# Drain buffers of one bank, one-hots in groups of tiles, and the order of loads and stores in a chunked attention with a mixture of experts

## The chip, the cores and the metric

One NeuronCore of a Trainium2 chip runs the whole program. The metric is the device time of one launch in microseconds (us), the median of several runs. Engines are named TensorE (PE; its weight loads PEld), VectorE (DVE), ScalarE (ACT), GpSimd (POOL) and SyncE (SP, which issues most of the DMAs). [...]

## The reference

Attention within chunks of 64 positions, for 8 batches, 8 heads, 576 positions and 64 dimensions; then a mixture of 8 experts over the 4608 tokens of 512 columns, for those tokens whose skip score is positive. Each token goes to its best expert alone:

```python
scores = scale * np.matmul(q_c, k_c.transpose(0, 1, 2, 4, 3))
attn = softmax(scores); x = np.matmul(attn, v_c)      # to (4608, 512)
xc = x[x @ w_skip > 0]
e_idx = np.argmax(xc @ w_gate, axis=1); gate_w = softmax(xc @ w_gate)[e_idx]
for e in range(8):
    h = np.maximum(xc[e_idx == e] @ w1[e], 0.0)       # 512 -> 1024
    y[e_idx == e] = gate_w * (h @ w2[e])              # 1024 -> 512
out = x.copy(); out[skip > 0] = xc + y
```

## The kernel before, in words

[...]

**Attention.** A loop (line 611) runs over 36 tiles of 128 tokens as a pipeline: in step i the scores of tile i+1 are computed (`pe_scores`, line 203) and their maximum taken (`ve_max`, line 214), tile i gets its exponential, tile i-1 its transpose and its product with v, tile i-2 its normalisation into x (line 258), tile i-3 is transposed again, scaled by ScalarE (line 290) and split into two float16 halves by GpSimd (`xh`, lines 292 and 293), and tile i-4 gets its routing logits on TensorE (lines 306 and 307). x is stored to `out` by SP (line 264); the stores of tiles from 23 on are held back until steps 34 and 35 and the code after the loop.

**Routing.** The tiles form three groups of 14, 9 and 13. When a group's logits are complete, a generator (`route`, line 323) yields its steps: kind "d" are VectorE steps with a cost, of which the loop takes some each tile (900 or 1100 ns, line 633), kind "p" TensorE steps. Each tile's one-hot of slots `oh` (line 396, VectorE, 128 x 128) and its record values `rv` (line 395, GpSimd; 88 columns a tile) go into matmuls that add up each expert's row records (line 413); `ohb` (line 387) is the one-hot of blocks. After group 1 the first three row blocks of the first expert are final and are gathered early by GpSimd's indirect DMA (line 470); after group 2 the rest.

**Weights.** W1 and W2 of the first expert come in 16 halves of 128 x 512 float32 (`load_half`, line 452), issued by SP in the steps that `W_TILES` (line 49) names: the eight halves of W1 in steps 23 to 30, those of W2 from 32 on. They pass through eight staging buffers (`wst`). `conv_half` (line 459) makes two float16 parts: ScalarE the first (line 462), GpSimd the second (a scaling, line 466, and a subtraction, line 467). Line 641 converts a half one step or more after it came. The other experts' weights are fetched four chunks ahead by `feed_load` (line 584; the DMA stands in line 576) through the same staging buffers, and converted by ScalarE and VectorE (lines 735 and 736).

**The drain.** After the loop (lines 650 to 714) the last tiles' steps are interleaved with the first layer of the first expert's first three blocks: `piece` (line 597) issues twelve matmuls over 384 columns for one eighth of the hidden columns, `evac` (line 604) its evacuation by ScalarE (line 495) and VectorE (line 496). Their PSUM comes from `sp_bank` (line 562), which hands out the two halves of tiles `sp` of two banks; two such tiles exist, shared with the scores of the loop. `early_xt` (line 568) transposes a gathered block. Before that code, line 650 calls `feed_load` once, ahead of the last five stores of x (lines 662 to 672). Lines 696, 697 and 704 to 706 are the last group's routing.

**The experts.** Units of row blocks follow, one expert after the other: layer two of a unit (line 520), with the next unit's gathers, transposes (line 483) and weights between its steps, then layer one of the next (line 491). Results are scattered by GpSimd (line 470).

Of the kernel before, what the change touches and what calls it, by code (L numbers as in the profile page):

```python
# [9 lines left out]
F32 = mybir.dt.float32  # L10
# [4 lines left out]
ALU = mybir.AluOpType  # L15
AX = mybir.AxisListType
PSUM = bass.MemoryType.PSUM

P = 128
# [4 lines left out]
DM = H * D  # L24
# [14 lines left out]
NG = len(GS)  # L39
# [3 lines left out]
NB = len(FLAT)  # L43
# [2 lines left out]
EMPTY = 5120.0  # L46

LOOK = 4
W_TILES = (23, 24, 25, 26, 27, 28, 29, 30, 32, 33, 33, 34, 34, 34, 35, 35)
W_ORDER = tuple((fc, part) for part in range(2) for fc in range(FC))  # L50
WSETS = 3
STB = 8
# [45 lines left out]
def moe_attention_kernel(ctx: ExitStack, tc: tile.TileContext, q: bass.AP, k: bass.AP, v: bass.AP, cst: bass.AP, wall: bass.AP, out: bass.AP):  # L98
    nc = tc.nc
    halves = (slice(0, CH), slice(CH, P))  # L100

    cpool = ctx.enter_context(tc.tile_pool(name="cpool", bufs=1))
# [2 lines left out]
    spool = ctx.enter_context(tc.tile_pool(name="spool", bufs=3))  # L105
    apool = tc.tile_pool(name="apool", bufs=2)
    ap = apool.__enter__()
    spool_ = tc.tile_pool(name="ps_s", bufs=2, space=PSUM)
    ps_s = spool_.__enter__()
    ppool = tc.tile_pool(name="ps_p", bufs=1, space=PSUM)  # L110
    ps_p = ppool.__enter__()

    man = tc.manual_schedule()
    man.__enter__()
# [51 lines left out]
    def C(name):  # L166
        lo, hi = _C[name]
        return csb[:, lo:hi]

    upper = cpool.tile([P, P], F16, name="upper")  # L170
    iota = cpool.tile([P, P], F16, name="iota")
# [5 lines left out]
    wgs = cpool.tile([P, KC, 2, NX], F16, name="wgs")  # L177
    reci = cpool.tile([P, NB], I32, name="reci")
    recg = cpool.tile([P, NB], F32, name="recg")
    onesf = cpool.tile([P, P], F32, name="onesf")  # L180
    nc.gpsimd.memset(onesf, 1.0)
    fixed = cpool.tile([P, 2, max(GS)], F32, name="fixed")
    nc.gpsimd.memset(fixed[:, 0], 1.0 / SGATE)
    nc.gpsimd.memset(fixed[:, 1], -0.498)
# [1 line left out]
    def more_constants():  # L186
        nc.vector.tensor_copy(upper, C("upper"))
        nc.vector.tensor_copy(iota, C("iota"))
        nc.vector.tensor_scalar(wgs[:, :, 0], wg, SR, None, op0=ALU.mult)
        nc.vector.scalar_tensor_tensor(wgs[:, :, 1], wg, SR, wgs[:, :, 0], op0=ALU.mult, op1=ALU.subtract)  # L190
        nc.gpsimd.tensor_copy(vals[:, :, 0], C("tok"))
        nc.gpsimd.tensor_copy(vals[:, :, 2], C("part").to_broadcast([P, NT]))
        nc.gpsimd.memset(ecum[:, 0, :], 0.0)
        nc.gpsimd.memset(rec, 0.0)
# [117 lines left out]
    def ve_logits(t):  # L312
        g, i, n = GT[t]
        if i == 0:
            lgs[g] = spool.tile([P, n, NX], F32, name="lg", bufs=3)
        nc.vector.tensor_reduce(lgs[g][:, i, :], T[t].pop("lp").rearrange("p (z n) -> p n z", z=2), axis=AX.X, op=ALU.add)
        if i == n - 1:
            r = route(g)
            routes.append([next(r), r])
# [3 lines left out]
    def route(g):  # L323
        n, t0 = GS[g], sum(GS[:g])
# [24 lines left out]
        vt = vals[:, t0:t0 + n, :]  # L349
# [31 lines left out]
        sl = spool.tile([P, n], F32, name="sl", bufs=2)  # L381
# [4 lines left out]
        ohb = ap.tile([P, n, NB], F16, name="ohb", bufs=2)  # L386
        nc.vector.scalar_tensor_tensor(ohb, C("kblk").unsqueeze(1).to_broadcast([P, n, NB]), 0.0, key.unsqueeze(2).to_broadcast([P, n, NB]), op0=ALU.add, op1=ALU.is_equal)
        rv = ap.tile([P, n, 4, NB], F16, name="rv", bufs=2)
        oh = ap.tile([P, n, P], F16, name="oh", bufs=2)
        for i in range(n):  # L390
            yield "d", 200
            s = slice(i, i + 1) if g + 1 < NG else slice(i, min(i + 7, n))
            sv = [P, s.stop - i, 4, NB]
            if g + 1 < NG or i % 7 == 0:
                nc.gpsimd.tensor_tensor(rv[:, s], ohb[:, s].unsqueeze(2).to_broadcast(sv), vt[:, s, :].unsqueeze(3).to_broadcast(sv), op=ALU.mult)
            nc.vector.scalar_tensor_tensor(oh[:, i, :], C("iota"), sl[:, i:i + 1], onesf, op0=ALU.is_equal, op1=ALU.mult)  # L396

        def sums():
            yield "d", 190
# [52 lines left out]
    def load_half(m):  # L452
        fc, part = W_ORDER[m]
        r = slice(part * DM, (part + 1) * DM)
        st = stpool.tile([P, DM], F32, name="wst")
        nc.sync.dma_start(st, wall[ORDER[0], fc, :, r])
        w_pend.append((st, fc, r))

    def conv_half(eng=nc.gpsimd):
        st, fc, r = w_pend.pop(0)  # L460
        w = wsets[0]
        nc.scalar.activation(w[:, 0, fc, r], st, AF.Copy, scale=SW)
        if eng is nc.vector:
            eng.scalar_tensor_tensor(w[:, 1, fc, r], st, SW, w[:, 0, fc, r], op0=ALU.mult, op1=ALU.subtract)
        else:
            eng.tensor_scalar(st, st, SW, 1.0, op0=ALU.mult, op1=ALU.mult)
            eng.tensor_tensor(w[:, 1, fc, r], st, w[:, 0, fc, r], op=ALU.subtract)
# [66 lines left out]
    def on(f, t, *a):  # L534
        if 0 <= t < NT:
            f(t, *a)
# [20 lines left out]
        for m in range(min(EARLY_B, ready[-1])):  # L557
            fetch(m, P * sum(GS[:EARLY_G]))

    spare = []  # L560

    def sp_bank():
        if not spare:
            t = ps_s.tile([P, 2, DM], F32, name="sp")
            spare.extend((t[:, 0], t[:, 1]))
        return spare.pop(0)

    def early_xt(m, alloc):
        blk_xt(xt0[:, :, :, m * P:(m + 1) * P], xgs[m], P, alloc)
# [1 line left out]
    def load_chunk(e, fc):  # L571
        st = [stpool.tile([P, DM], F32, name="wst") for _ in range(2)]
        for part in range(2):
            r = slice(part * DM, (part + 1) * DM)
            src = wall[e, fc, :, r] if isinstance(e, int) else wall[bass.ds(e, 1), fc, :, r].rearrange("o p w -> (o p) w")
            nc.sync.dma_start(st[part], src)
        return st
# [6 lines left out]
    def feed_load():  # L584
        while queue and len(pend) < STB // 2:
            p, fc = queue[0]
            if p >= WSETS and last[p - WSETS] >= unit[0]:
                return
            queue.pop(0)
            pend.append((p, fc, load_chunk(ORDER[p], fc)))  # L590
# [6 lines left out]
    def piece():  # L597
        if todo:
            fc = todo.pop(0)
            hp = sp_bank()[:, :N0]  # L600
            l1_mm(xt0, wsets[0], N0, hp, fc)
            evs.append((hp, fc))
# [8 lines left out]
    for i in range(-1, NT):  # L611
        host.clear()
        if i >= 0:
            on(load_q, i + LOOK)
            on(load_k, i + LOOK)
        for m in [m for m, t in enumerate(W_TILES) if t == i]:
            load_half(m)
# [21 lines left out]
        if i == 1:  # L639
            more_constants()  # L640
        if w_pend and (i > W_TILES[FC] or i < W_TILES[FC] and (len(w_pend) > 1 or i > W_TILES[FC - 1])):
            conv_half()
# [4 lines left out]
            run_route("rd", 1 << 30)  # L647
        early_fetch()

    feed_load()  # L650


    def conv():
        if w_pend:
            conv_half()

    host.clear()
    pe_ptrans(NT - 1)
    pe_xtrans(NT - 3, sp_bank)
    ve_norm(NT - 2)  # L660
    ac_pt(NT - 1)
# [5 lines left out]
    pe_logits(NT - 4)  # L667
    ve_logits(NT - 4)
    early_xt(EARLY_B - 1, sp_bank)
    pe_pv(NT - 1)  # L670
    ve_norm(NT - 1)
# [40 lines left out]
        evac()  # L712
    while w_pend:
        conv()
    apool.__exit__(None, None, None)
    ppool.__exit__(None, None, None)
    spool_.__exit__(None, None, None)
    bpool = ctx.enter_context(tc.tile_pool(name="bpool", bufs=1))
    ps_h = ctx.enter_context(tc.tile_pool(name="ps_h", bufs=3, space=PSUM))
    ps_x = ctx.enter_context(tc.tile_pool(name="ps_x", bufs=2, space=PSUM))  # L720
    ps_y = ctx.enter_context(tc.tile_pool(name="ps_y", bufs=3, space=PSUM))

    def xq_bank():
        return ps_x.tile([P, DM], F32, name="xq")
# [93 lines left out]
    for u, (p, bs, offs, n) in enumerate(units):  # L818
# [7 lines left out]
        w, hc = wsets[p], ht  # L826
# [38 lines left out]
    with tc.For_i(0, lend, 1) as si:  # L865
# [8 lines left out]
        for t in range(NT):  # L874
            oh = spool.tile([P, P], F16, name="ohx", bufs=2)
# [48 lines left out]
```

## Time and profile before

| | |
|---|---|
| median of 3 runs | 381.53 us (380.94 to 382.79) |
| the profiled execution, its own time | 381.37 us |
| its span | 379.6 us |
| TensorE busy | 327.1 us (86%) |
| VectorE, ScalarE, GpSimd busy | 245.6, 165.3, 152.2 us |
| mean granted clock of TensorE | 0.958 |
| moved by DMA | 81.83 MB, 216 GB/s on the mean |

All the views are of one profiled execution. The span runs from the first to the last instruction; the time also holds what lies around it. Busy shares are means over stages with different limits: the loop over tiles ends near 145 us, the drain near 182 us, the experts fill the rest. In a row of the timeline "[1.84 <-X]" says that the engine had been idle for 1.84 us and that X released it; "issue" is idle time for which the profile shows no releaser. SPq is SP's queue.

### The profile page before, as it was taken

What the parts mean: (1) busy time and instruction counts of PE and PEld (TensorE: products, weight loads), DVE (VectorE), ACT (ScalarE), POOL (GpSimd) and SP (SyncE); (2) the same over time, 40 slices, a digit from 0 to 9 for tenths busy, and PEclk for the clock granted to TensorE, in tenths of its full rate; (3) what the DMA queues carried; (4) which work ended last, traced back from release to release, by engine and by line L of the source; (5) the groups of instructions that cost most, each with busy time, mean ns of one, the idle gap of its engine ahead of it and who ended that gap; (6) DMA issues with size and microseconds to landing.
All of it is one profiled execution on the core that took longest, in us unless ns stands there. A gap on an engine that the chain in (4) does not pass through costs nothing.

```text
span 379.6 us, 11266 instructions
## 1 busy us (share of the span) xinstructions
PE 327.1 (86%) x4543; PEld 230.5 (61%) x4543; DVE 245.6 (65%) x552; ACT 165.3 (44%) x335; POOL 152.2 (40%) x195
## 2 busy tenths in 40 slices
PE   7777777878886767687999999899999999999991
PEld 3667666767775655453455555485674766769570
DVE  1554445779669826457554799887697777966520
ACT  2443433544555435321433572366365454645320
POOL 5154453568889986441712012502423124011111
PEclk9998998999989889986999999999999999999997
DMA  7999898998987961114474258767657867575000
GB/s 276 392 374 322 238 271 292 273 298 281 385 294 226 328 232 59 55 56 167 159 235 154 72 205 272 254 222 229 230 172 233 262 212 239 190 216 168 29 26 26
DMA packets 42472, 81.83 MB, mean 216 GB/s; under 512 B 5150, under 2 KB 5150, under 8 KB 42416
## 3 DMA queue, kind: packets, MB, share of 16 engines
q1 hardware_dynamic: 39168, 71.47, 57.0%
q0 software_dynamic: 3104, 9.33, 7.5%
q8 instruction: 37, 0.61, 0.6%
q10 hardware_dynamic: 144, 0.26, 0.2%
q14 instruction: 19, 0.16, 0.1%
HBM read 67.01 MB, written 14.17 MB: 214 GB/s over the span
## 4 chain that ended last, share of the span: by engine, by line
PE 70%; DVE 15%; issue 6%; ACT 4%; POOL 1%; DMA 1%; POOLq 0%; ACTq 0%; DVEq 0%
PE y L520 25%; PE hp L491 19%; PE sp L211 5%; DVE oh L396 5%; PE sp L491 4%; PE xt L279 4%; PE pv L248 4%; ACT xs L290 3%; PE xq L483 2%; DVE mx L216 2%; PE pt L233 2%; PE xt L306 2%; PE xt L162 1%; PE sp L222 1%; DVE x L258 1%
## 5 line engine op out<-in xcount | busy, mean ns | idle before, releaser
L520 PE MATMUL y<-wset,ht 128*128 128x512 f16 (+7 forms) x552 | 101.9, 379 | 0.0
L491 PEld LDWEIGHTS <-wset 128*128 128x128 f16 x864 | 74.9, 99 | 32.2 <-issue 12.8
L491 PE MATMUL hp<-xt,wset 128*128 128x288 f16 (+6 forms) x768 | 81.1, 267 | 1.8 <-DVE ht L496 1.1
L470 POOL DMA_INDIRECT out<-yo,reci x22 | 24.5, 1112 | 142.7 <-DVE yo L530 122.7
L520 PEld LDWEIGHTS <-ht 128*128 128x128 f16 (+7 forms) x552 | 45.6, 101 | 46.5 <-issue 2.0
L736 DVE SCALAR_TENSOR_TENSOR wset<-wst,wset 128x512 f16<-128x512 f32 x112 | 71.5, 683 | 1.4 <-ACT wset L735 0.8
L735 ACT ACTIVATE wset<-wst 128x512 f16<-128x512 f32 x112 | 63.0, 621 | 2.0 <-DMA wst<-in_wall 2.0
L290 ACT ACTIVATE xs<-xt 128x512 f32<-128x512 f32 x33 | 19.7, 596 | 61.3 <-PE xt L279 58.8
L495 ACT ACTIVATE ht<-hp 128x288 f16<-128x288 f32 (+6 forms) x64 | 23.6, 370 | 49.7 <-PE hp L491 49.4
L216 DVE TENSOR_REDUCE mx<-sp 128x8 bf16<-128x512 f32 x36 | 24.7, 687 | 24.9 <-PE sp L211 24.9
L496 DVE SCALAR_TENSOR_TENSOR ht<-hp,ht 128x288 f16<-128x288 f32 (+6 forms) x64 | 25.2, 404 | 22.6 <-ACT ht L495 21.5
L293 POOL TENSOR_TENSOR xh<-xs,xh 128x512 f16<-128x512 f32 x33 | 38.2, 1157 | 2.7
L292 POOL CAST xh<-xs 128x512 f16<-128x512 f32 x33 | 20.4, 617 | 42.3 <-ACT xs L290 42.2
L248 PE MATMUL pv<-v,pts 64*64 64x65 f32 x1152 | 27.4, 228 | 8.5 <-issue 8.1
L211 PE MATMUL sp<-qk 64*64 64x64 f32 x1152 | 27.7, 234 | 5.2 <-issue 4.6
L470 POOL DMA_INDIRECT xg<-out,reci x22 | 24.7, 1123 | 14.4 <-DMA out<-x 8.1
L248 PEld LDWEIGHTS pv<-v,pts 64*64 64x64 f32 x1152 | 23.1, 141 | 9.8 <-issue 9.2
L211 PEld LDWEIGHTS sp<-qk 64*64 64x64 f32 x1152 | 22.2, 143 | 8.5 <-issue 6.4
L484 ACT ACTIVATE xt<-xq 128x512 f16<-128x512 f32 (+7 forms) x19 | 9.6, 508 | 40.9 <-PE xq L483 40.9
L226 ACT ACTIVATE px<-sp 128x512 f32<-128x512 f32 x36 | 21.6, 600 | 11.5 <-PE sp L222 11.5
L258 DVE TENSOR_TENSOR x<-pv,rr 128x512 f32<-128x512 f32 x36 | 24.9, 691 | 1.2
L233 PE MATMUL pt<-ident,px 128*128 128x128 f32 x144 | 23.7, 291 | 1.4 <-ACT xs L290 1.4
(123 smaller groups left out, 387.5 us busy)
## 6 DMA issues: line engine op xcount, KB each, us to landing
wst<-in_wall SPq DMA_DIRECT2D x128, 256.0 KB, 3.6
v<-in_v SPq DMA_DIRECT2D x36, 260.0 KB, 4.6
qk<-in_q SPq DMA_DIRECT2D x36, 256.0 KB, 4.8
out<-x SPq DMA_DIRECT2D x36, 256.0 KB, 5.1
qk<-in_k SPq DMA_DIRECT2D x35, 256.0 KB, 5.3
xg<-out,reci POOLq DMA_INDIRECT x22, 5.3
out<-yo,reci POOLq DMA_INDIRECT x22, 4.0
qk<-in_k ACTq DMA_DIRECT2D x1, 256.0 KB, 3.8
```

Source lines behind the costliest of these rows:

```text
L211: nc.tensor.matmul(sp[halves[a], c, j * CH:(j + 1) * CH], qk[halves[c], 0, w], qk[halves[c], 1, w], start=(j == 0), stop=False, skip_group ...
L216: nc.vector.tensor_reduce(mx, T[t]["sp"][:, :, :KC * CH].rearrange("p c (j s) -> p c j s", s=CH), axis=AX.X, op=ALU.max, negate=True)
L233: nc.tensor.transpose(pt[:, j, :], px[:, j * P:(j + 1) * P], ident)
L248: nc.tensor.matmul(pv[halves[c], jj, m * VW:(m + 1) * VW], pt[halves[jj], c * 2 + jp, halves[a]], vv[halves[jj], c * KC + m, :], start=(m ...
L258: nc.vector.tensor_tensor(x.rearrange("p (g m d) -> p g m d", g=2, m=KC), pv[:, :, :, :D], rr.unsqueeze(3).to_broadcast([P, 2, KC, D]), op ...
L290: nc.scalar.activation(xs, T[t].pop("xt"), AF.Copy, scale=SX)
L293: nc.gpsimd.tensor_tensor(xh[:, 1], xs, xh[:, 0], op=ALU.subtract)
L470: ins = nc.gpsimd.indirect_dma_start(**kw)
L491: nc.tensor.matmul(hp, w[:, a, fc, j * P:(j + 1) * P], xt[:, b, j, :n], start=(m == 0), stop=(m == 11))
L520: nc.tensor.matmul(y[c * P // cg:c * P // cg + n], ht[:, a, fc, o:o + n], w[:, b, fc, P * KC:], start=(f == 0 and m == 0), stop=(f == fw - ...
L735: nc.scalar.activation(w[:, 0, fc, r], st[part], AF.Copy, scale=SW)
L736: nc.vector.scalar_tensor_tensor(w[:, 1, fc, r], st[part], SW, w[:, 0, fc, r], op0=ALU.mult, op1=ALU.subtract)
```

## The change

`sp_bank` takes its PSUM from a new pool of four tiles of one bank, `pd`, opened after the loop in the place of the pool of `sp`; the pool of `xt`, `pt` and `pv` is opened first so that it can outlive it, and the experts' pools are opened in another order (so in other banks). One-hots and record values are made for three tiles by one operation each, for seven in the last group, with an iota spread over the tiles instead of a scalar operand and the tile of ones. The call of `feed_load` ahead of the last stores is gone; the next call stands behind the last store. The eight halves of W1 are loaded in steps 6, 9, ... 27; line 641 then converts one in steps 9, 12, ... 27 and the last in step 28.

```diff
-W_TILES = (23, 24, 25, 26, 27, 28, 29, 30, 32, 33, 33, 34, 34, 34, 35, 35)
+W_TILES = (6, 9, 12, 15, 18, 21, 24, 27, 32, 33, 33, 34, 34, 34, 35, 35)
...
+    ppool = tc.tile_pool(name="ps_p", bufs=1, space=PSUM)
+    ps_p = ppool.__enter__()
     spool_ = tc.tile_pool(name="ps_s", bufs=2, space=PSUM)
     ps_s = spool_.__enter__()
-    ppool = tc.tile_pool(name="ps_p", bufs=1, space=PSUM)
-    ps_p = ppool.__enter__()
...
-    onesf = cpool.tile([P, P], F32, name="onesf")
-    nc.gpsimd.memset(onesf, 1.0)
...
-        for i in range(n):
-            yield "d", 200
-            s = slice(i, i + 1) if g + 1 < NG else slice(i, min(i + 7, n))
-            sv = [P, s.stop - i, 4, NB]
-            if g + 1 < NG or i % 7 == 0:
-                nc.gpsimd.tensor_tensor(rv[:, s], ohb[:, s].unsqueeze(2).to_broadcast(sv), vt[:, s, :].unsqueeze(3).to_broadcast(sv), op=ALU.mult)
-            nc.vector.scalar_tensor_tensor(oh[:, i, :], C("iota"), sl[:, i:i + 1], onesf, op0=ALU.is_equal, op1=ALU.mult)
+        step = 3 if g + 1 < NG else 7
+        for i in range(0, n, step):
+            s = slice(i, min(i + step, n))
+            w = s.stop - i
+            yield "d", 60 + 133 * w
+            sv, so = [P, w, 4, NB], [P, w, P]
+            nc.gpsimd.tensor_tensor(rv[:, s], ohb[:, s].unsqueeze(2).to_broadcast(sv), vt[:, s, :].unsqueeze(3).to_broadcast(sv), op=ALU.mult)
+            nc.vector.scalar_tensor_tensor(oh[:, s, :], C("iota").unsqueeze(1).to_broadcast(so), 0.0, sl[:, s].unsqueeze(2).to_broadcast(so), op0=ALU.add, op1=ALU.is_equal)
...
-    spare = []
-
     def sp_bank():
-        if not spare:
-            t = ps_s.tile([P, 2, DM], F32, name="sp")
-            spare.extend((t[:, 0], t[:, 1]))
-        return spare.pop(0)
+        return dpool.tile([P, DM], F32, name="pd")
...
-    feed_load()
+    spool_.__exit__(None, None, None)
+    dpool_ = tc.tile_pool(name="ps_d", bufs=4, space=PSUM)
+    dpool = dpool_.__enter__()
...
+    dpool_.__exit__(None, None, None)
+    ppool.__exit__(None, None, None)
     apool.__exit__(None, None, None)
-    ppool.__exit__(None, None, None)
-    spool_.__exit__(None, None, None)
     bpool = ctx.enter_context(tc.tile_pool(name="bpool", bufs=1))
+    ps_y = ctx.enter_context(tc.tile_pool(name="ps_y", bufs=3, space=PSUM))
+    ps_x = ctx.enter_context(tc.tile_pool(name="ps_x", bufs=2, space=PSUM))
     ps_h = ctx.enter_context(tc.tile_pool(name="ps_h", bufs=3, space=PSUM))
-    ps_x = ctx.enter_context(tc.tile_pool(name="ps_x", bufs=2, space=PSUM))
-    ps_y = ctx.enter_context(tc.tile_pool(name="ps_y", bufs=3, space=PSUM))
```

## Rows read from the trace of the kernel before

**Rows 1.** Busy time of each engine by stage: the stretch, its length, busy microseconds of PE, PEld, DVE, ACT and POOL with their instructions, then granted clock, DMA share and GB/s.

```profile
64.00:92.00 28.00, 23.12 (x639) 20.60 (x639) 22.65 (x64) 12.65 (x24) 17.53 (x30) 0.94 0.89 273
...
100.00:127.00 27.00, 19.74 (x521) 17.55 (x520) 22.05 (x59) 13.42 (x26) 24.27 (x35) 0.92 0.85 280
...
160.00:182.00 22.00, 17.26 (x88) 9.20 (x88) 13.59 (x39) 3.17 (x7) 8.15 (x10) 0.77 0.28 96
182.00:379.00 197.00, 186.82 (x1398) 117.87 (x1395) 136.80 (x253) 91.86 (x197) 44.83 (x40) 0.99 0.57 183
```

**Rows 2.** The chain that ended last, in order of time (start, length, what): its pieces on the one-hots of line 396.

```profile
83.41 0.94 DVE oh L396 x3
...
86.07 1.78 DVE oh L396 x5
...
89.57 1.94 DVE oh L396 x5
...
116.09 2.87 DVE oh L396 x5
...
120.68 3.05 DVE oh L396 x4
...
168.39 6.62 DVE oh L396 x13
```

**Rows 3.** Timeline of VectorE around `ohb` (start, length, operation), and the groups of `rv` on GpSimd by shape (count, busy us, mean ns).

```profile
81.97 1.43 DVE L387 SCALAR_TENSOR_TENSOR ohb<-csb,key 128x308 f16<-128x308 f32 x1
...
167.43 0.17 DVE L379 SCALAR_TENSOR_TENSOR bi<-rank,fixed 128x13 int32<-128x13 f32 x1
...
167.93 0.46 DVE L387 SCALAR_TENSOR_TENSOR ohb<-csb,key 128x286 f16<-128x286 f32 x1
...
L395 POOL TENSOR_TENSOR rv<-ohb,vals 128x88 f16<-128x88 f16 x23 | 7.9, 371 | 0.4 <-DVE ohb L387 0.4
...
L395 POOL TENSOR_TENSOR rv<-ohb,vals 128x616 f16<-128x616 f16 x1 | 1.2, 1212 | 3.9 <-DVE ohb L387 3.9
```

**Rows 4.** Timeline of GpSimd at the early gathers, and of TensorE at the logits behind them.

```profile
128.34 0.62 POOL L466 TENSOR_SCALAR wst<-wst 128x512 f32<-128x512 f32 x1
129.04 1.16 POOL L467 TENSOR_TENSOR wset<-wst,wset 128x512 f16<-128x512 f32 x1
130.37 1.26 POOL L470 DMA_INDIRECT xg<-out,reci  x1 [0.18 <-DVE ecum L427]
...
134.27 0.63 POOL L292 CAST xh<-xs 128x512 f16<-128x512 f32 x1
...
134.95 0.18 PE L306 MATMUL xt<-wgs,xh 128*128 128x18 f16 x1 [2.74 <-POOL xh L292]
136.18 0.19 PE L307 MATMUL xt<-wgs,xh 128*128 128x9 f16 x1 [1.05 <-POOL xh L293]
```

**Rows 5.** Timeline of TensorE in the drain, and VectorE's row for the block indicator `eh` of the last group.

```profile
148.83 0.66 PE L483 MATMUL sp<-ident,xg 128*128 128x128 f32 x4 [1.34 <-DVE xh L287]
...
154.81 2.11 PE L491 MATMUL sp<-xt,wset 128*128 128x384 f16 x12 [1.84 <-DVE ht L496]
...
162.65 3.28 PE L491 MATMUL sp<-xt,wset 128*128 128x384 f16 x12 [2.96 <-DVE ht L496]
165.73 0.31 PE L363 MATMUL xt<-eh,upper 128*128 128x117 f16 x1
...
166.57 4.20 PE L491 MATMUL sp<-xt,wset 128*128 128x384 f16 x24
...
172.96 2.36 PE L413 MATMUL xt<-rv,oh 128*128 128x88 f16 x9 [1.03 <-DVE oh L396]
175.53 6.49 PE L491 MATMUL sp<-xt,wset 128*128 128x384 f16 x24 [0.21 <-DVE ht L496]
181.85 3.40 PE L520 MATMUL y<-wset,ht 128*128 128x512 f16 x15
...
161.85 0.28 DVE L346 SCALAR_TENSOR_TENSOR eh<-csb,val 128x117 f16<-128x117 f32 x1
```

**Rows 6.** TensorE's waits for "issue" from 20 to 130 us (who waited for what: us in total, times, longest us), and the timeline's row of one of them.

```profile
PE pv L248 <- issue: 8.1, 6, 2.0
PE sp L211 <- issue: 4.6, 4, 1.9
...
101.11 0.34 PE L248 MATMUL pv<-v,pts 64*64 64x65 f32 x7 [1.10 <-issue]
```

**Rows 7.** Busy time by stretch in the drain, columns as in rows 1.

```profile
170.00:174.00 4.00, 2.16 (x13) 1.03 (x11) 4.00 (x8) 0.49 (x1) 2.59 (x3) 0.96 0.04 3
174.00:180.00 6.00, 5.75 (x21) 2.61 (x21) 3.52 (x14) 0.49 (x1) 0.00 (x0) 0.50 0.73 263
```

**Rows 8.** Timeline of SP's queue, of GpSimd and of ScalarE around the last stores and the gathers of the remaining blocks.

```profile
139.88 33.23 SPq L576 DMA_DIRECT2D wst<-in_wall  x8
173.20 2.79 SPq L264 DMA_DIRECT2D out<-x  x5
...
180.89 1.06 POOL L470 DMA_INDIRECT xg<-out,reci  x1 [8.13 <-DMA out<-x]
...
193.99 0.44 ACT L484 ACTIVATE xt<-xq 128x320 f16<-128x320 f32 x1 [7.22 <-PE xq L483]
```

## The prediction

> **What bounds the kernel now.** I read the busy time by stage first, then the chain of waits, then the timeline of each engine where the chain leaves TensorE. From 182 us on TensorE is busy 187 of 197 us [rows 1]: that half is bound by its matmuls, and nothing in the change shortens them. Before 182 us it is not: 17.3 of 22 us are busy from 160 to 182, and part of that at the lower clock (granted 0.77 on the mean) [rows 1]. Time can be won only there. The chain says what stands in the way: the one-hots of line 396 on VectorE in three places [rows 2], GpSimd from 100 to 127 us (24.3 of 27 us busy [rows 1]), and in the drain TensorE's waits for VectorE's evacuations [rows 5]. By half a per cent (1.9 us) and less this kernel's runs cannot be told from no change.
>
> **The sum's base.** The profiled execution took 381.4 us (span 379.6, 1.8 outside); the median of the three runs is 381.5, so I subtract from 381.4 and compare with either.
>
> **(a) One-hots of group 0, attention stage.** Fourteen operations become five (3, 3, 3, 3, 2 tiles). On the chain thirteen of the old ones took 0.94 + 1.78 + 1.94 = 4.66 us [rows 2], so fourteen some 5.0. The new form is that of `ohb` (an iota spread over one axis, a value over the other): 286 columns took 0.46 us, a 13-column operation 0.17 [rows 3], hence 0.17 us plus 1.06 ns a column. Three tiles are 384 columns, 0.56 us; two are 0.43. Five operations: 2.7 us, a gain of 2.3 if none is stopped. But an operation of VectorE with two SBUF inputs can stand behind GpSimd: `ohb` with 308 columns took 1.43 us while a subtraction of `xh` ran beside it [rows 3], 0.9 more than its own 0.5. I take 1.5 saved (0 to 2.3), nearer the free end because fewer operations meet fewer of GpSimd's.
>
> **(b) One-hots of group 1.** Nine in 2.87 + 3.05 = 5.92 us [rows 2]; they stood behind the W1 conversions too. Three new ones are 1.7 us of their own; with two stops of 0.6 they are 2.9. Saved 3.0 (1.2, if all three are stopped for 1.0, to 4.2). `rv` in threes on GpSimd goes from nine times 0.37 to three times 0.65 (88 columns 0.37, 616 columns 1.21, so 1.6 ns a column [rows 3]), 1.4 us less on the engine that is full there.
>
> **(c) W1's conversions leave GpSimd's full stretch.** Eight times 0.62 + 1.16 = 14 us of GpSimd move from tiles 24 to 31 to tiles 9 to 28 (one half every third tile, behind its load), where GpSimd was busy 17.5 of 28 us [rows 1]. What ends: the last conversion of W1 (until 130.2) stands ahead of the early gathers, which occupy GpSimd until 134.3, so the cast for tile 29 starts at 134.27 and TensorE's logits wait 2.74 + 1.05 us [rows 4]. With the gathers some 2 us and more earlier against the tiles, about 1 us of that wait is left. Saved 2.8 (0 to 3.8). In the tiles that now get a conversion, the cast of the next tile may start up to a microsecond late; a tile's logits follow one tile later, which covers that. Without the cover it would cost a microsecond in each of eight tiles.
>
> **(d) W1's loads at tiles 6 to 27.** Eight loads of 256 KB, each with one more issue in SP's queue, ahead of a store and of a load of v that is asked for four tiles early: nothing. They add 2.1 MB over some 80 us, 26 GB/s on 273 [rows 1]. What could pay is TensorE's stalls on "issue" in the middle of a run of matmuls, 8.1 + 4.6 us in ten places from 20 to 130 us [rows 6]: if each load lengthens one by its own transfer (256 KB at 300 GB/s, 0.87 us), 7 us; if they hide as the eight at tiles 23 to 30 did, 0, and those go away. I take 1.0 lost (0 to 7): the stall at 101 us, among the loads of before, was 1.10 us, no longer than others [rows 6]. [...]
>
> **(e) Drain: waits that come from shared tiles.** `sp_bank` deals out two halves of a two-bank tile. Three times TensorE waited to write one half until VectorE had read the other: 1.34 us at 148.83 (`early_xt` after the evacuation of tile 33's transpose), 1.84 at 154.81 (piece 1 after the evacuation of piece 0), 2.96 at 162.65 (piece 3 after that of piece 2) [rows 5]. With four tiles of one bank, a write waits only for the reader four calls back, which is long past in every case (piece 4 reuses piece 0's). The first two delay everything behind them: saved 3.2. The third stands in front of the ranking matmuls: `eh` is ready at 162.13, they start at 165.73, after the wait and a piece at half clock (3.28 us, against 2.11 at 154.81) [rows 5]. Freed, piece 3 runs while VectorE routes and is over when `eh` is. Saved 3.6.
>
> **(f) One-hots of the last group.** From the first operation at 168.4 [rows 2] to the last record matmul at 175.3 [rows 5] it is 6.9 us, 6.6 of them thirteen operations. Two operations of 896 and 768 columns are 1.11 and 0.97 us, GpSimd's two `rv` 1.21 and (528 columns, by the slope) 1.07 [rows 3]. Fully beside each other they need 2.3 us, one after another 4.4; the `ohb` row says that they stop each other, so I take 4.2, and 0.6 for the last six matmuls: 4.8. Saved 2.1 (1.9 to 4.0). GpSimd's last W2 conversion then comes behind both `rv`; the matmuls of layer two need it some 8 us later.
>
> **(g) Clock.** After the empty stretches before 162.6 and between 170 and 174 (2.2 of 4 us busy) the granted clock was 0.50, and pieces 6 and 7 took 6.49 us instead of the 4.20 of pieces 4 and 5 [rows 5, 7]. With (e) and (f) one gap of about 1.5 us is left ahead of the record matmuls. I take 1.5 of the 2.3 us (0 to 2.3).
>
> **(h) Stores ahead of the next expert's loads.** Eight loads sat in SP's queue for 33 us, waiting for staging buffers, and five stores behind them went out only at 173.2; the gathers then waited 8.1 us for the stores [rows 8]. Now the stores go as soon as x is there, and the loads queue behind the last of them. Saved on the chain: nothing. ScalarE had waited 7.2 us for the transposes of those gathers when they came at 193.99 [rows 8], because TensorE had layer two to do. The loads' price: the first of them move back behind the last store, the last still waits for the last conversion of W2, so all are on their way before layer two begins, and ScalarE converts from there on. If that cover failed, the conversions would start late by one landing: the last store was out by 176.0 and held the gather until 180.9, so some 5 us.
>
> **(i) Banks, `onesf`.** The later pools get the same numbers of banks; 0 (1 either way).
>
> Sum: attention -1.5 - 3.0 - 2.8 + 1.0 = -6.3; drain -3.2 - 3.6 - 2.1 - 1.5 = -10.4; in all -16.7, so **364.7 us**, 4.4% faster. All the rest moves earlier as a block.
>
> **Rivals.** *Drain only:* the attention stage gives its gain back, because TensorE's own tile with a stall is as long as the tiles that (a) to (c) shorten, or because (d) costs its upper bound. For: GpSimd and VectorE can take turns stopping each other with long operations as with short ones. Against: the chain runs through line 396 there [rows 2]. 381.4 - 10.4 = 371.0. *The change doesn't do what it says in the drain:* the waits of (e) belong to the order of the evacuations, not to the sharing of a tile, and come back on the new buffers with the clock. Against: pieces 4 and 5, which have no evacuation between them in program order, ran on without a wait in one tile [rows 5]. 381.4 - 6.3 - 2.1 = 373.0. *Slower:* the loads of (d) meet nearly full transfer queues (0.89 busy [rows 1]) and every code stall grows. To undo 16.7 and lose 2 more, each of the ten must grow by 1.9 us, from 1.3 to 3.2, and the price then is 384. It decides only beyond twice the mean stall; the longest of before is 2.0 [rows 6], with loads or without.
>
> **Chances.** Forecast (357 to 370) 0.66; drain only 0.15; waits stay 0.09; slower 0.06; nothing measurable 0.04. The first three are faster: 0.90; same 0.04; slower 0.06. All the terms at their good ends would give 358, at their bad ends 378; 357 to 374 takes in the forecast and the first two rivals and leaves out about 0.15.
>
> **What would show it.** Right: the waits of TensorE for line 496 before pieces 1 and 3 gone; five, three and two one-hot operations of about 0.56 and 1.0 us plus their stops; the gathers by 122 and the logits behind them waiting about 1 us; the first layer-two matmul near 165 instead of 181.85, at full clock; no gather waiting for `out`. Wrong: tiles 6 to 27 longer by more than 2 us in sum, pieces still waiting, or layer two starting later than 172.

## The result, and the profile after

| | before | after |
|---|---|---|
| median, with the result | 381.24 us (378.55 to 382.79) | 368.01 us (367.01 to 369.15) |
| ratio, with the result | | 0.966 [0.960, 0.973] |
| ratio, in two later sets of runs | | 0.955 [0.948, 0.961] and 0.956 [0.949, 0.962] |
| median of all 16 runs of after | | 366.6 us (362.3 to 369.2) |
| the profiled execution, its time and span | 381.37, 379.6 us | 367.09, 365.3 us |
| exponential of tile 35 begins | 144.70 us | 140.22 us |
| first matmul of layer two | 181.85 us | 167.43 us |
| from there to the end | 197.75 us | 197.87 us |

The kernel became 3.4 to 4.5% faster; 364.7 us was predicted and 366.6 is the median. The medians are of all executions; the ratios leave out those more than 1.5% above the fastest of their kernel. The rows of after have other line numbers, most of them two less: 209 and 246 are scores and product with v, 290 and 291 the float16 halves, 394 and 395 record values and one-hots, 469 gathers, 490 layer one, 519 layer two.

All of the profiled gain, 14.3 us, lies ahead of layer two, as forecast: 4.5 us until tile 35's exponential and 9.9 us from there to the first matmul of layer two (37.15 us before, 27.21 after). After that nothing changed (+0.1). Two later profiles of the same kernel divide the gain otherwise: 3.1 and 2.6 us until tile 35's exponential, and 12.3 from there to layer two (24.85 us).

Busy time by stage of the kernel after, columns as in [rows 1]:

```profile
64.00:92.00 28.00, 23.07 (x639) 20.60 (x632) 22.85 (x59) 13.29 (x26) 20.45 (x25) 0.94 0.92 302
100.00:127.00 27.00, 22.34 (x617) 19.68 (x608) 21.05 (x63) 12.64 (x24) 21.30 (x26) 0.94 0.80 262
136.00:140.00 4.00, 2.97 (x27) 2.65 (x27) 1.06 (x3) 0.88 (x2) 1.60 (x2) 0.54 0.52 199
140.00:146.00 6.00, 5.73 (x77) 4.79 (x78) 2.49 (x7) 3.33 (x7) 3.09 (x4) 0.50 0.20 74
146.00:167.00 21.00, 18.84 (x185) 12.43 (x178) 15.99 (x42) 7.45 (x16) 14.29 (x16) 0.99 0.34 107
167.00:365.00 198.00, 187.24 (x1401) 118.13 (x1399) 136.26 (x252) 91.33 (x196) 44.63 (x40) 0.99 0.56 183
```

GpSimd has 3.0 us less to do from 100 to 127 and 2.9 more from 64 to 92, and TensorE is busy 22.3 of those 27 us, no longer 19.7. In this profile the drain from 146 on runs at a granted clock of 0.99, where [rows 7] had 0.50; the low stretch now lies ahead of it, from 136 to 146 (0.54 and 0.50). The granted clock is TensorE's, as the share of its full speed that the profile gives; in the traces of before and after it is 1.00 or 0.50 at every moment from 7 us on, and a figure between them is a mean.

The chain that ended last, its rows on record values and one-hots and at its end (start, length, what), against [rows 2]:

```profile
83.37 1.78 POOL rv L394 x2
...
86.94 1.80 POOL rv L394 x2
...
114.94 2.31 DVE oh L395 x2
...
159.43 2.89 DVE oh L395 x2
...
163.69 3.90 PE pd L490 x24
167.59 11.65 PE y L519 x54
```

The one-hots of group 0 are off the chain, and GpSimd's record values (`rv`) have their place. The last group's one-hots fell from 6.62 to 2.89 us.

Timeline of TensorE, against [rows 4, 5]; the fourth row is a product with v that waited for "issue":

```profile
128.51 0.18 PE L304 MATMUL xt<-wgs,xh 128*128 128x18 f16 x1 [0.31 <-POOL xh L290]
...
129.75 0.18 PE L305 MATMUL xt<-wgs,xh 128*128 128x9 f16 x1 [1.05 <-POOL xh L291]
...
137.03 0.70 PE L246 MATMUL pv<-v,pts 64*64 64x65 f32 x12 [2.27 <-issue]
...
149.30 2.11 PE L490 MATMUL pd<-xt,wset 128*128 128x384 f16 x12
...
154.04 2.11 PE L490 MATMUL pd<-xt,wset 128*128 128x384 f16 x12
156.64 0.21 PE L361 MATMUL xt<-eh,upper 128*128 128x117 f16 x1 [0.49 <-DVE eh L344]
...
163.53 4.07 PE L490 MATMUL pd<-xt,wset 128*128 128x384 f16 x24
```

Pieces 1 and 3 (149.30 and 154.04) start without a wait; the ranking starts 0.06 us after `eh` is ready, not 3.6; pieces 6 and 7 take 4.07 us, not 6.49. Of the logits' wait behind the early gathers, 2.74 + 1.05 us, 0.31 + 1.05 is left.

Timeline of GpSimd, of SP's queue and of ScalarE, against [rows 4, 8]:

```profile
123.93 1.26 POOL L469 DMA_INDIRECT xg<-out,reci  x1 [0.32 <-DVE recg L434]
...
165.37 1.06 POOL L469 DMA_INDIRECT xg<-out,reci  x1 [0.16 <-DVE recg L434]
...
128.84 19.66 SPq L262 DMA_DIRECT2D out<-x  x9
148.59 51.34 SPq L570 DMA_DIRECT2D wst<-in_wall  x21
...
179.56 0.44 ACT L483 ACTIVATE xt<-xq 128x320 f16<-128x320 f32 x1 [8.31 <-PE xq L482]
```

The first early gather went from 130.37 to 123.93 (127.36 and 127.65 in the two later profiles); here it waits for the routing, no longer behind W1. The stores leave ahead of the loads, and the gather of the remaining blocks waits 0.16 us, not 8.13. ScalarE then waits 8.31 us for TensorE, where it waited 7.22: the earlier gathers bring nothing, as the forecast had it.

### The profile page after: what moved, and what is told of

It reads as the page before. It is cut to its first block, busy times and chain, and to the rows that moved or that the text cites. A ratio compares the mean times of both kernels' runs of the same rounds, so it can differ in the third digit from the quotient of the medians.

```text
span 365.3 us, 11225 instructions
## 1 busy us (share of the span) xinstructions
PE 322.1 (88%) x4543; PEld 229.2 (63%) x4543; DVE 237.7 (65%) x526; ACT 165.0 (45%) x335; POOL 152.8 (42%) x179
## 4 chain that ended last, share of the span: by engine, by line
PE 74%; DVE 9%; issue 7%; ACT 4%; POOL 4%; DMA 1%; POOLq 0%; ACTq 0%; DVEq 0%
PE y L519 26%; PE hp L490 20%; PE sp L209 5%; PE pv L246 5%; PE xt L277 4%; ACT xs L288 3%; PE pd L490 3%; PE xq L482 2%; PE xt L304 2%; PE pt L231 2%; DVE oh L395 1%; PE xt L162 1%; PE sp L220 1%; DVE mx L214 1%; DMA xg<-out,reci 1%
## 5 line engine op out<-in xcount | busy, mean ns | idle before, releaser
L490 PEld LDWEIGHTS <-wset 128*128 128x128 f16 x864 | 73.5, 98 | 24.2 <-issue 3.8
L288 ACT ACTIVATE xs<-xt 128x512 f32<-128x512 f32 x33 | 19.7, 596 | 58.7 <-PE xt L277 56.6
L246 PE MATMUL pv<-v,pts 64*64 64x65 f32 x1152 | 28.2, 230 | 8.7 <-issue 8.1
L224 ACT ACTIVATE px<-sp 128x512 f32<-128x512 f32 x36 | 21.6, 599 | 10.3 <-PE sp L220 10.2
```

Source lines behind the costliest of these rows:

```text
L246: nc.tensor.matmul(pv[halves[c], jj, m * VW:(m + 1) * VW], pt[halves[jj], c * 2 + jp, halves[a]], vv[halves[jj], c * KC + m, :], start=(m ...
L288: nc.scalar.activation(xs, T[t].pop("xt"), AF.Copy, scale=SX)
L490: nc.tensor.matmul(hp, w[:, a, fc, j * P:(j + 1) * P], xt[:, b, j, :n], start=(m == 0), stop=(m == 11))
```

## The experiments

The runs came in three sets, one under each of the next three headings, and each ratio is against the kernel before in the same set. The kernel after itself was run in the second set (label after_again: 364.71 us, 0.955 [0.948, 0.961]) and in the third (after_third: 366.59 us, 0.956 [0.949, 0.962]), not in the first.

### One part undone at a time

**u_banks**: the new pool, but two tiles of two banks dealt out in halves.

```diff
     def sp_bank():
-        return dpool.tile([P, DM], F32, name="pd")
+        if not spare:
+            t = dpool.tile([P, 2, DM], F32, name="pd")
+            spare.extend((t[:, 0], t[:, 1]))
+        return spare.pop(0)
...
-    dpool_ = tc.tile_pool(name="ps_d", bufs=4, space=PSUM)
+    dpool_ = tc.tile_pool(name="ps_d", bufs=2, space=PSUM)
```

> The changed kernel, with the drain's buffers again two tiles of two banks, each dealt out in halves. Theory (sharing a tile makes TensorE wait for the other half's reader): the waits before early_xt, piece 1 and piece 3 are back (1.3, 1.8 and 3.0 us) and the lower clock with them, 6 to 8 us slower than the changed kernel, about 375 us. Rival (the waits belong to the order of the evacuations): the same 368 us.

Measured: 373.07 us, 0.975 [0.968, 0.981]. Timeline of TensorE at `early_xt`, at pieces 1 and 3 and at layer two:

```profile
148.03 0.66 PE L482 MATMUL pd<-ident,xg 128*128 128x128 f32 x4 [1.34 <-DVE xh L285]
...
154.01 3.79 PE L490 MATMUL pd<-xt,wset 128*128 128x384 f16 x12 [1.83 <-DVE ht L495]
...
163.54 3.18 PE L490 MATMUL pd<-xt,wset 128*128 128x384 f16 x12 [2.97 <-DVE ht L495]
...
177.16 11.82 PE L519 MATMUL y<-wset,ht 128*128 128x512 f16 x54
```

All three waits [rows 5] are back, to a hundredth, with all the rest of the change in place, and every execution is longer than the six of after_again on the same chip (370.86 us or more against 366.74 or less). The waits belong to the sharing of a tile, not to the order of the evacuations.

**u_onehot**: the old one-tile one-hots and the tile of ones (the part of the change's diff on them, with its signs turned).

> The changed kernel with one one-hot operation a tile again (and the tile of ones). Theory: the last group's one-hots cost 2.7 us more on the chain, those of group 1 about 2 us, those of group 0 nothing; 4 to 6 us slower, about 373 us. Rival (grouping pays only where nothing else of VectorE waits, in the last group): 2.7 us, 370.7 us.

Measured: 371.22 us, 0.972 [0.965, 0.979]. Timelines of VectorE and of TensorE in the drain:

```profile
158.45 6.70 DVE L396 SCALAR_TENSOR_TENSOR oh<-csb,sl,onesf 128x128 f16<-128x128 f32 x13
...
165.25 6.06 PE L491 MATMUL pd<-xt,wset 128*128 128x384 f16 x24
171.14 11.82 PE L520 MATMUL y<-wset,ht 128*128 128x512 f16 x54
```

From tile 35's exponential (141.67) to layer two it is 29.47 us, against 24.85 in after_again and after_third: 4.6. About 2.7 us of it are the one-hots, and 2.0 come in pieces 6 and 7, which take 6.06 us instead of 4.07; the kernel before had 6.49 for them, at a granted clock of 0.50 [rows 7]. Tile 35's exponential itself is no later than in the kernel after (140.22 to 142.08): in groups 0 and 1 the old operations cost nothing that shows.

**u_w1**: `W_TILES` as before.

> The changed kernel with W1 loaded in steps 23 to 30 again, so converted in steps 24 to 31. Theory (the eight conversions on GpSimd hold up tiles 27 to 34): 4 to 6 us slower at step 34, 1.5 us of it given back in tiles 6 to 23; about 371.5 us. Rival (the one-hots in groups alone shortened those tiles): the same 368 us or a microsecond less.

Measured: 368.30 us, 0.965 [0.958, 0.971]. Tiles 27 to 35 (from exponential to exponential) take 36.99 us, against 31.1 to 33.6 in the eight profiles that convert W1 early: the conversions cost there what the theory said. Tiles 5 to 27 took 78.14 us, the shortest of all thirteen profiles (less_dma, below, aside), which more than gives it back; but that execution (364.4 us) was also the fastest of its six, and by the ratio u_w1 is some 3 us behind the kernel after.

**u_order**: `feed_load()` ahead of the last stores again.

> The changed kernel with the next expert's first eight loads issued ahead of the last stores again. Theory (the stores' place saves nothing on the chain, and the stores now fill the transfer queues while TensorE's code is fetched: a stall of 2.3 us at 137 us and the lower clock until 147): 2 to 5 us faster, about 364.5 us, and the stall of 137 us gone. Rival (the late stores held the gathers, and these the experts): 4 us slower, 372 us.

Measured: 365.15 us, 0.956 [0.950, 0.962], and 24.85 us from tile 35 to layer two. The order of stores and loads makes no difference that these runs can tell. Theory and rival fell: the time is that of the kernel after, and a stall at tile 34 is still there, 0.80 us long.

### What W1's place is worth, and the stall at tile 34

**after_again** is the kernel after.

> The changed kernel unchanged, as the measure for the other runs here and to see whether its stalls come at the same places in a second profile. Theory: about 368 us, and TensorE stalls on issue for about 2 us in the product with v of tile 34 again. Rival (the stall at 137 us was chance): no stall there, and the time spreads over 364 to 371 us.

Measured: 364.71 us (362.33 to 366.74), and the stall at tile 34 is there again, 1.32 us long.

**stored29**: the stores held back from tile 29 on, not from 23.

```diff
-STORED = 23
+STORED = 29
```

> The changed kernel with only the stores of tiles from 29 on held back (before: from 23 on); six stores move into steps 26 to 31, ahead of the loads of W2. Theory (TensorE's code stands behind the backlog of stores in the transfer queues at 128 to 137 us): the queues are empty earlier, no stall in tile 34's product with v and no lower clock until 147; 4 us faster than the changed kernel, about 364 us. Rival (the place of the stall is not set by the stores): the same as the changed kernel, or slower by what the six stores cost in tiles 26 to 31.

Measured: 365.25 us, 0.951 [0.944, 0.958]. The timeline of TensorE:

```profile
139.81 0.45 PE L246 MATMUL pv<-v,pts 64*64 64x65 f32 x12 [1.49 <-issue]
```

The stall ahead of tile 34's product with v stayed (2.27 us in the first profile of after, 1.32 in after_again, 1.49 in after_third), though fewer stores are held back until then. Their place doesn't set it; that theory fell.

**order_w1**: the order of the loads and `W_TILES` both as before.

```diff
-W_TILES = (6, 9, 12, 15, 18, 21, 24, 27, 32, 33, 33, 34, 34, 34, 35, 35)
+W_TILES = (23, 24, 25, 26, 27, 28, 29, 30, 32, 33, 33, 34, 34, 34, 35, 35)
...
+    feed_load()
```

> The changed kernel with the next expert's loads ahead of the last stores again and W1 in steps 23 to 30 again, so with only the buffers and the one-hots changed. Theory (W1's place gives in tiles 27 to 34 what it takes in tiles 6 to 27): as fast as with the order alone undone, about 364.5 us. Rival (the two interact: W1's late loads make the backlog of the stores longer): 3 us slower than that.

Measured: 370.35 us (366.52 to 375.05), 0.966 [0.957, 0.974], some 4 us above u_order by the ratio. The theory that W1's place gives back what it takes fell; and since u_w1, with the new order, is at 0.965, the order adds nothing to it.

**loads_only**: W1 loaded in tiles 6 to 27, but converted in tiles 24 to 31.

```diff
-        if w_pend and (i > W_TILES[FC] or i < W_TILES[FC] and (len(w_pend) > 1 or i > W_TILES[FC - 1])):
+        if w_pend and (i > 32 or 24 <= i < 32):
```

> The changed kernel with W1 loaded in steps 6 to 27 but converted in steps 24 to 31, as before. Theory (tiles 6 to 27 pay for the loads, by TensorE's stalls on code, and tiles 27 to 34 for the conversions on GpSimd): it pays both, 3 to 5 us slower than the changed kernel, about 372 us. Rival (the early conversions are what tiles 6 to 27 pay for): as W1 late, about 368 us.

Measured: 370.64 us (369.22 to 373.51), 0.972 [0.966, 0.979]. Timelines of GpSimd and of TensorE, and last TensorE's wait of 129.06 as after_again has it:

```profile
129.08 1.16 POOL L466 TENSOR_TENSOR wset<-wst,wset 128x512 f16<-128x512 f32 x1
130.42 1.26 POOL L469 DMA_INDIRECT xg<-out,reci  x1 [0.18 <-DMA wst<-in_wall]
...
134.32 0.63 POOL L290 CAST xh<-xs 128x512 f16<-128x512 f32 x1
...
129.06 0.38 PE L220 MATMUL sp<-mx,identb 128*128 128x256 bf16 x2 [2.04 <-DVE mx L214]
...
135.00 0.18 PE L304 MATMUL xt<-wgs,xh 128*128 128x18 f16 x1 [2.92 <-POOL xh L290]
...
136.23 0.19 PE L305 MATMUL xt<-wgs,xh 128*128 128x9 f16 x1 [1.05 <-POOL xh L291]
...
128.47 0.38 PE L220 MATMUL sp<-mx,identb 128*128 128x256 bf16 x2 [0.46 <-DVE mx L214]
```

This separates loading from converting. All six runs are longer than all six of after_again on the same chip (362.33 to 366.74), and the medians are 5.9 us apart: converting early is what W1's place brings. The rows at the gathers are those of [rows 4] again, to 0.2 us. Loading early by itself brings nothing: order_w1, which loads late, is at 0.966, and the intervals overlap. In the profiles layer two starts at 170.42 and 170.94 us in these two, and at 166.50 in after_again.

### Single parts, and code against transfers

**after_third** is the kernel after.

> The changed kernel once more, as the measure for this set: between 364 and 368 us.

Measured: 366.59 us (362.87 to 368.26), as expected.

**last7**: groups 0 and 1 tile by tile, the last group in sevens.

```diff
-        step = 3 if g + 1 < NG else 7
+        step = 1 if g + 1 < NG else 7
```

> The changed kernel with groups 0 and 1 in operations of one tile (new form) and only the last group in sevens. Theory (the chain through the one-hots in tiles 28 to 32 was VectorE and GpSimd stopping each other once a pair): 3 to 4 us slower than the changed kernel, most of it in tiles 27 to 33. Rival (those tiles were held by the conversions of W1 alone, and the one-hots pay in the last group alone): the same time as the changed kernel.

Measured: 365.88 us, 0.955 [0.949, 0.961], the same as the kernel after. One-hots and record values of group 1 in its timeline, of VectorE and of GpSimd:

```profile
116.11 2.74 DVE L395 SCALAR_TENSOR_TENSOR oh<-csb,sl 128x128 f16<-128x128 f32 x5
120.49 1.75 DVE L395 SCALAR_TENSOR_TENSOR oh<-csb,sl 128x128 f16<-128x128 f32 x3
...
117.99 1.63 POOL L394 TENSOR_TENSOR rv<-ohb,vals 128x88 f16<-128x88 f16 x5
```

Eight one-hots take 4.49 us here. The same group's three operations took 2.31 us (the first two, on the chain above) and 0.55 in the kernel after:

```profile
118.89 0.55 DVE L395 SCALAR_TENSOR_TENSOR oh<-csb,sl 128x384 f16<-128x384 f32 x1
```

The grouping spares VectorE 1.6 us and the ninth operation, and the end does not move: in these tiles that work does not set the time.

**banks_only**: the kernel before with the one-bank buffers and the order of the pools, and nothing else.

> The kernel before with the one-bank buffers (and the order of the pools) alone. Theory (the waits on the other half are 6 to 8 us with their clock, whatever the rest): 6 to 8 us faster than before. Rival (without the shorter one-hots the last group's routing takes the gain back, since TensorE then waits there): 3 us or less.

Measured: 375.59 us, 0.979 [0.972, 0.985], 8 us by the ratio: the theory held. The timeline of TensorE, pieces 1, 3, 6 and 7:

```profile
151.54 2.11 PE L491 MATMUL pd<-xt,wset 128*128 128x384 f16 x12
...
156.28 2.11 PE L491 MATMUL pd<-xt,wset 128*128 128x384 f16 x12
...
168.38 6.71 PE L491 MATMUL pd<-xt,wset 128*128 128x384 f16 x24
174.93 11.82 PE L520 MATMUL y<-wset,ht 128*128 128x512 f16 x54
```

From tile 35's exponential (144.80) to layer two it is 30.13 us, 7.0 less than before. Pieces 6 and 7 are as slow as before (6.71 us, then 6.49), while u_banks, with the shorter one-hots but tiles shared in halves, has 4.07: these pieces are shortened by the one-hots, not by the buffers.

**less_dma**: odd tiles from 7 on take q, k and v of the tile before instead of loading their own; its time as a whole says nothing, since the routing becomes another.

```diff
-        if t < NT:
+        if t > 5 and t % 2 and t < NT:
+            T[t]["qk"] = T[t - 1]["qk"]
+        elif t < NT:
```

> The changed kernel with the loads of q, k and v left out in every odd tile from 7 on (the tile before it is used again, so its x and the routing differ and the time after the attention stage says nothing). Theory (TensorE's stalls on issue are its code standing behind data in the transfer queues): with three eighths of the traffic gone the stalls after tile 7 fall from some 12 us to under 4, and the exponential of tile 27 comes by 100 us instead of 107 to 110. Rival (a stall is a fixed cost of passing from one block of code to the next): the stalls stay at 1 to 2.5 us each, at the same matmuls.

Busy time from 30 to 100 us, of after_third and then of less_dma:

```profile
30.00:100.00 70.00, 56.22 (x1503) 49.79 (x1502) 41.98 (x114) 32.01 (x61) 45.11 (x54) 0.90 0.91 294
```

```profile
30.00:100.00 70.00, 60.31 (x1756) 52.92 (x1755) 50.71 (x137) 37.87 (x73) 52.87 (x63) 1.00 0.73 246
```

TensorE's waits in that stretch (who waited for what: us in total, times, longest), of after_third and then of less_dma:

```profile
PE sp L209 <- issue: 5.3, 3, 3.4
PE pv L246 <- issue: 3.0, 2, 2.2
PE xt L277 <- issue: 2.0, 1, 2.0
```

```profile
PE pv L250 <- issue: 2.3, 4, 1.1
PE sp L213 <- issue: 0.6, 1, 0.6
```

With the transfers' share down from 0.91 to 0.73, TensorE's stalls on "issue" fall from 10.3 to 2.9 us, the granted clock is 1.00 instead of 0.90, and tile 27's exponential begins at 97.9 us, where after_third has 110.6. In these two profiles the stalls are larger with more transfers beside them; the rival of a fixed cost for each fell, since no stall of this stretch is longer than 1.1 us in less_dma, against 3.4 in after_third.

The packets of an instruction queue come ahead of these stalls. This is the queue's row in the profile of the kernel after (packets, MB, share); the trace also has the times of each packet:

```profile
q8 instruction: 37, 0.61, 0.6%
```

From 20 to 145 us all the fourteen profiles together have 145 stalls of TensorE on "issue". Of these, 138 end 1.2 to 1.7 us after a packet of this queue has landed, all ten of the kernel before and all twelve of the first profile of after among them (1.26 to 1.58 us); with some 21 packets in that stretch of each profile, about one in ten would by chance (an estimate from these counts). By that the stalls are taken here for waits on TensorE's code. Eight to 13 stalls come to 20 to 23 packets (ten to 22 before, twelve to 21 after): about half of the packets have no stall behind them.

## Why the prediction held, step by step

The sum was -16.7, and the runs give -13 to -17 (0.966 to 0.955). That it came so near is in part luck. The attention part was forecast at -6.3 and came to -4.5, -3.1 and -2.6 us in the three profiles of the kernel after; the drain was forecast at -10.4 and came to -9.9, -12.3 and -12.3. One error made up for the other. The mechanisms held in the drain; the attention part gained by other terms than the forecast named. Layer two was forecast to begin near 165 us and began between 164.4 and 167.4 in the profiles of the changed kernel and of those as fast.

**(e) The shared tiles: right.** Predicted -6.8. The three waits are gone after, all three return in u_banks, and the buffers alone make the drain 7.0 us shorter (8 by the ratio of banks_only). The rival that the waits belong to the order of the evacuations fell.

**(f), (g) The last one-hots and the clock: right, a little small.** Predicted -2.1 and -1.5. From the end of `ohb` to the last record matmul it is 4.26 us (159.43 to 163.69), 6.93 before: -2.7. The two operations and GpSimd's `rv` hold each other up, as assumed from the `ohb` row [rows 3] (1.43 us there): they take 2.97 and 3.67 us. Timelines of VectorE and GpSimd of the kernel after:

```profile
156.30 0.28 DVE L344 SCALAR_TENSOR_TENSOR eh<-csb,val 128x117 f16<-128x117 f32 x1
...
158.97 0.46 DVE L385 SCALAR_TENSOR_TENSOR ohb<-csb,key 128x286 f16<-128x286 f32 x1
159.34 2.97 DVE L395 SCALAR_TENSOR_TENSOR oh<-csb,sl 128x896 f16<-128x896 f32 x2
...
159.57 3.67 POOL L394 TENSOR_TENSOR rv<-ohb,vals 128x616 f16<-128x616 f16 x2 [0.49 <-DVE ohb L385]
```

The first row is `eh`, from whose end the ranking's 0.06 us is counted. By the slopes of [rows 3], an estimate, the last two needed 2.1 and 2.3 us each for themselves, 4.4 one after another; together they end after 3.9. The clock's part is put at 2.0 to 2.4 us, by pieces 6 and 7: 6.49 us before, at a granted clock of 0.50 [rows 7], and 6.06 in u_onehot, against 4.07 after, where it is 0.99. In sum the drain is 12.3 us shorter in after_again and after_third (24.85 against 37.15), where 10.4 was predicted. In the first profile it is only 9.9: there the granted clock stood at 0.50 from 136 to 146, about the stall of 2.27 us that ended at 137.03, where after_third has 1.00.

**(a), (b) One-hots of groups 0 and 1: the step that failed.** Predicted -1.5 and -3.0. Group 1's operations did become 3.1 us shorter (5.92 to 2.86), just the size forecast, but last7, which has them tile by tile, is as fast as the kernel after, and u_onehot, with the old operations, reaches tile 35's exponential as early. The forecast took their place on the chain of waits [rows 2] for their worth. The chain says what was last at each step; what is next behind it the rows of that chain don't say. In group 0 it was GpSimd's `rv`, 1.78 and 1.80 us in the chain after; the forecast had named this itself as what speaks for the rival, and for these tiles that rival was true.

**(c) W1's conversions: right in kind, half the size.** Predicted -2.8, which came out of one wait, that for the gathers [rows 4]. Measured by loads_only against after_again: -5.9 in the times, -3.9 in the profiles (layer two at 170.42 and 166.50). Tiles 27 to 35 take 37.97 and 31.23 us, 6.7 less, and two tiles hold it. From tile 33's exponential to tile 34's it is 8.49 and 4.36 us: the gathers' wait is 2.92 us against 0.44, and behind it, at 136.51, the 32 matmuls of a tile's scores take 1.13 us in loads_only, where they took 0.69 at 129.64 (the granted clock is 0.87 in the mean from 120 to 141). From tile 31's to tile 32's it is 6.20 and 3.44: TensorE waits 2.04 us for `mx`, against 0.46. VectorE comes late to it: of its routing steps there, one of 128x3 (`reci`) took 0.74 us in the kernel before, beside a W1 subtraction of GpSimd, and 0.24 in the first profile of the kernel after. The forecast priced the conversions at the gathers alone and put the rest of these tiles' time down to (b). Tiles 5 to 27, where the conversions now lie, take 83.70 and 86.24 us, 2.5 more; yet that stretch spreads from 83.8 to 86.8 us among kernels that are alike up to there, and from 78.1 to 85.3 among those that convert late, so what the conversions cost there is not shown.

**(d) W1's loads: little, the size open.** Predicted +1.0 (0 to 7). loads_only loads early, order_w1 and u_w1 load late, and all three convert late: 0.972, 0.966 and 0.965, with overlapping intervals. That fits 0 to 3 us; 7 was not reached. (The 300 GB/s behind that 7 was the forecast's estimate; 273 GB/s at a DMA share of 0.89 [rows 1] come to 307.) TensorE's stalls on "issue" from 30 to 130 us come to 10.0 to 12.6 us in the four profiles that load late and 10.7 to 14.1 in the nine that load early: 1.1 more in the mean, within the spread. One of the forecast's own signs of being wrong did come: tiles 6 to 27, from exponential to exponential, took 79.40 us before and 80.96, 83.45 and 82.81 in the three profiles after. Four kernels that load and convert late spread from 75.35 to 82.50 over the same tiles, so the runs do not say whether the loads, the conversions or neither did that. About half of the code packets have a stall behind them, single stalls last up to 3.4 us (after_third), and in less_dma their sum from 30 to 100 us is 7.4 us smaller, at a DMA share of 0.73 instead of 0.91. So the rival that every stall grows with the traffic is borne out by less_dma, but eight loads of 256 KB did not move the stalls beyond their spread.

**(h), (i): right.** u_order shows no difference; the later pools' banks show none after 167 us (187.24 us busy in 198, before 186.82 in 197).

**What the forecast had not seen** is the stall at tile 34. It is in six of the eight profiles that convert W1 early (0.80 to 2.31 us), each time ahead of the last twelve matmuls of the product, and in none of the five that convert late. In four of the five the logits of the tile before wait long for the gathers (2.92 + 1.05 us in loads_only), and no stall follows at tile 34; the two early profiles without the stall, u_banks and u_onehot, have a wait of 2.87 us for ScalarE's `xs` in tile 32. That such waits cover it fits these six. But u_w1 has 1.07 + 0.43 us there, no more than after_again with 0.44 + 1.05, so what places the stall stays open. Nor is there a version clearly faster than the change: stored29, u_order and last7 lie within its interval.

## What to carry to other kernels

A row on the chain of waits is not yet the worth of shortening it: (b) was credited with 3.0 us by that chain, and undoing the grouping there cost nothing. The chain says what ended last, not what ends next behind it; so undo the piece alone before crediting it. Work that is moved off a full engine can be worth more than the one wait that names it: 6.7 us in the tiles that W1's conversions left, where the wait for the gathers accounts for 2.5. A wait of a matmul for a reader of the other half of its own two-bank tile is cheap to find and to remove: here it was half of the gain (7.0 us in banks_only, of 14.3).

## What the runs showed of the hardware

TensorE's stalls on "issue" end 1.2 to 1.7 us after a packet of the instruction queue has landed (138 of 145), and their sum was smaller with fewer transfers beside them: 10.3 us in 70 at a DMA share of 0.91 (after_third), 2.9 at 0.73 (less_dma). The granted clock of that stretch was 0.90 and 1.00. VectorE's one-hots took longer beside GpSimd's work than the slope of [rows 3] gives (an estimate), as few long operations (2.97 us for 2.1, with `rv` at 3.67 for 2.3, 3.9 for both) and as many short ones (eight one-hots in 4.49 us for 2.4, in last7). And the same program differs from run to run by 6.9 us (362.3 to 369.2 over 16 runs), and from tile 5 to 27 by 2.5 us in three profiles of the kernel after (83.75 to 86.24), so terms of a microsecond in that stage could be read from the rows only where a wait names them.
